# An attention chain with expert routing: rows of x spread by way of DRAM, masks and shares in fewer transfers, part of the first batch on GpSimd, and a new order of work

## The chip, the core and the metric

The kernel runs on one of the eight cores of a Trainium2 chip. A core has five engines that run side by side, each through its own queue in order: TensorE (PE, matrix products; its weight loads are shown as PEld), VectorE (DVE), ScalarE (ACT), GpSimd (POOL) and SyncE (SP), which here issues nearly all the transfers (DMAs). Matrix products land in PSUM, eight banks of 128 x 512 floats; everything else lies in SBUF, 128 rows wide, or in DRAM. The metric is the time of one execution in microseconds (us) of device time; smaller is better.

## The reference

Two blocks follow each other. The first is linear attention with a sketched feature map; its output, with the heads side by side, is the input x of the second, four attention experts of which each token uses two.

```python
# q, k, v: (4 batches, 4 heads, 1088, 32); S1, S2: (8, 32)
phi(x) = outer(S1 @ x, S2 @ x)                     # 64 features per head and row
kv, z  = phi(k)^T @ v, sum(phi(k))
x      = (phi(q) @ kv) / (phi(q) @ z + 1e-6)       # (4, 1088, 128)

logits = x @ w_gate                                # 4 experts
top 2 of each row, w = softmax over those two
for e in range(4):
    a   = softmax(causal((x @ wq[e]) @ (x @ wk[e])^T / 8))
    out += (w of e, or 0) * (a @ (x @ wv[e]) @ wo[e])
```

S1 and S2 come in float64 and are split into two floats at the start.

## The kernel before

The 1088 rows of a batch are nine tiles of 128 (the last has 64). Query times key of an expert is folded into one 128 x 128 matrix per expert (`mcat`), value times output into `mo`, so an expert's scores are x · mcat[e] · x^T. Each row uses two experts, so a tile makes two score rows per token (two "slots"); which expert stands in which slot is a mask, broadcast over all 128 rows of SBUF because the selection runs along the columns. The tiles 0 to 3 are kept in reversed 32-row groups (`BACK`).

There is no automatic scheduling: the text `ORDER` is the program. It is a list of words `batch.task[:arguments]`, executed top to bottom, and each engine's queue holds its instructions in that order. PSUM banks go to the least recently used one (`bank`), with some held over several tasks. A word that needs a result waits on its engine's queue, and everything behind it waits too. The words that matter:

- `ld` loads k, q and v of a batch; `bk`, `bq` transpose k and q on VectorE (for batch 0 the query in halves, `bq0`, `bq1`); `vk` copies the values of batch 0 into `vp`.
- `ks`, `qs` are the sketches: matmuls, a copy on ScalarE, a product. In batch 0 (`first_sketch`, L340) the product reads PSUM and runs on VectorE (L364); in the others it runs on GpSimd (L393).
- `kv` sums the features of k times the values; `tf` turns the query features on PE; `nu` (L415) divides and writes `xs`, one buffer that all batches share; `tx` turns `xs` into `xT` on PE.
- `em`, `eo` fold the expert matrices; `warm` gives PE filler matmuls.
- `ga` computes the gate logits and the selection; `ge` and `gw` the weights. `md` (`spread_masks`, L503) turns the selection, writes it to DRAM (`dm`) and broadcasts it to `mk`. `mp` (`masks`, L522) makes masks of batch 0 on PE instead, before that broadcast is there.
- `cu` (`chosen`, L534) computes x · mcat for two tiles and lets VectorE pick each row's experts by mask (`uT`, L549).
- `s` are scores (L582; the last tile, `last_step`, L604), with mask and maximum on VectorE (L557) and exponentials on ScalarE (L561); `t` transposes the weights on VectorE (L271).
- `sp` (`spread_x`, L274) copies `xs` into `xrep`, which holds x in 32-row blocks, once in each quarter of the rows of SBUF; `vb` and `va` (L638) are the weighted sums over `xrep`, for the tiles 1 to 5 and for 0, 6, 7, 8, in four parts each.
- `shb`, `sha` (`shares`, L654) give the factors of the rows, written to DRAM and broadcast; `shp` does it on PE for the end.
- `zb` sorts the sums by expert (L711, L713), `o` multiplies by `mo` (L720), copies (L723) and stores.

The work of one batch is woven into that of the batch before, so that the start of batch 1 stands among the scores of batch 0. Scores of batch 0 begin after a long chain that has nothing to weave in: sketches, `kv`, `nu`, `tx`, gate, masks, `cu`.

Of the kernel before, what the change touches and what calls it, by code (L numbers as in the profile page):

```python
# [22 lines left out]
    0.bk 0.bq1 0.bq0 0.ks:4:9 0.ks:0:4 0.warm:2 0.qs:0:4 0.warm:2 0.vk 1.ld 0.qs:4:9 0.kv 1.bk 0.tf:0:8 0.warm:2 0.em  # L23
    0.nu:0:4 1.ks:0:4 1.bq 0.tf:13:18 0.tf:8:13 0.tx:0:4 1.ks:4:9 0.nu:4:9 0.eo 0.tx:4:9 0.ga:0:4 0.ge:0 0.gw:0
    0.ga:4:9 1.kv 0.mp:8:9 0.mp:2:4 2.ld 0.ge:4 0.mp:0:2 0.mp:6:8 0.mp:4:6 0.gw:4 2.bk 0.cu:2 1.qs:0:4 1.qs:4:9 0.cu:6
    0.md 0.cu:4 0.cu:0 0.cu:8 1.tf:0:8 1.tf:8:13 0.s:5:1 0.s:3 0.t:1 1.tf:13:18 0.t:5 2.ks:4:9 0.sp 2.ks:0:4 0.s:4:2
    0.s:7 1.nu:5:9 1.nu:0:5 0.shb 0.t:3 2.kv 1.tx:4:9 0.t:4 1.tx:0:4 0.s:8 0.t:2 0.t:7 1.ga:0:9 1.md 0.s:6:0 1.ge:0
    2.bq 0.vb:0 0.vb:1 0.vb:2 0.vb:3 0.zb:5 2.qs:4:9 2.qs:0:4 0.t:0 1.cu:2 0.t:8 0.o:5 1.cu:6 1.cu:4 1.cu:8 0.t:6
    1.cu:0 1.s:4:2 3.ld 3.bk 1.s:5:1 0.sha 0.va:0 0.va:1 1.t:5 2.tf:8:13 2.tf:13:18 0.va:2 1.gw:0 1.t:1 0.zb:3 0.va:3
    0.zb:6 1.sp 2.tf:0:8 1.t:2 1.t:4 1.s:6:0 0.o:3 1.s:3 0.zb:0 0.o:6 0.zb:1 1.s:7 0.o:0 1.t:3 0.o:1 2.nu:5:9 3.ks:4:9  # L30
    3.ks:0:4 2.nu:0:5 1.t:6 1.shb 1.t:7 1.vb:0 0.zb:8 2.tx:0:4 3.bq 2.tx:4:9 1.vb:1 1.vb:2 2.ga:0:9 2.md 2.ge:0 1.vb:3
    0.o:8 3.kv 1.zb:1 1.t:0 1.s:8 3.qs:4:9 3.qs:0:4 2.cu:0 1.o:1 1.t:8 2.cu:4 2.cu:6 1.sha 2.cu:2 2.s:5:1 2.gw:0
    1.zb:5 2.s:3 1.zb:3 1.va:0 1.va:1 2.t:1 1.va:2 1.va:3 1.o:5 3.tf:8:13 3.tf:0:8 2.t:3 3.tf:13:18 2.t:5 2.cu:8
    2.s:4:2 2.t:4 2.sp 1.o:3 2.t:2 2.s:7 2.s:8 1.zb:8 2.shb 3.nu:0:5 3.nu:5:9 1.zb:0 2.vb:0 2.vb:1 2.t:7 3.tx:0:4
    3.tx:4:9 2.vb:2 2.t:8 3.ga:0:9 1.o:8 1.zb:6 3.md 2.vb:3 1.o:0 2.zb:5 2.s:6:0 2.t:6 3.cu:4 1.o:6 2.o:5 3.cu:6
    3.cu:2 3.cu:0 2.zb:1 2.t:0 3.cu:8 3.s:4:2 3.ge:0 3.s:5:1 2.sha 3.t:2 2.zb:3 2.o:1 2.va:0 3.t:1 2.va:1 3.t:4 3.t:5
    2.va:2 2.va:3 2.zb:0 3.s:3 3.sp 3.s:6:0 3.t:0 3.t:3 2.o:3 3.s:7 2.zb:8 3.gw:0 3.shb 2.o:0 3.s:8 2.o:8 3.t:6 3.vb:0
    3.t:8 3.vb:1 3.t:7 3.vb:2 3.vb:3 3.zb:1 3.va:0 3.va:1 3.va:2 3.o:1 3.zb:3 3.shp 2.zb:6 3.va:3 3.o:3 2.o:6 3.zb:6
    3.o:6 3.zb:0 3.zb:5 3.o:0 3.o:5 3.zb:8 3.o:8
# [4 lines left out]
def kernel(  # L44
# [114 lines left out]
    for _ in range(4):  # L159
        nc.tensor.matmul(P[:, 7], idle, idle[:, None, :].to_broadcast([128, 4, 128]), start=True, stop=True)  # L160
# [113 lines left out]
    def spread_x(b):  # L274
        for s in range(4):
            nj = (NC - s + 3) // 4
            for r in range(4):
                nc.sync.dma_start(out=xrep[32 * r : 32 * r + 32, s : s + 4 * (nj - 1) + 1 : 4],  # L278
                                  in_=xs[32 * s : 32 * s + 32, 0:nj])
# [15 lines left out]
    class Batch:  # L295
# [5 lines left out]
        def __init__(self, b):  # L301
            self.b, self.ab, self.fp, self.uT = b, {}, {}, {}
            self.yT, self.qpT = yT, qpT
# [12 lines left out]
    def batch(b):  # L316
        if b not in made:
            made[b] = Batch(b)
        return made[b]
# [20 lines left out]
    def first_sketch(nm, j0, j1, eng):  # L340
# [8 lines left out]
        fp, k0, w = m_.fp[nm], bank(2), 2 * R * (j1 - j0)  # L349
        for j in range(j0, j1):  # L350
# [7 lines left out]
        for m in range(2):  # L358
# [4 lines left out]
            nc.scalar.copy(a, t[:, 0])  # L363
            eng.tensor_tensor(  # L364
                out=o, op=ALU.mult,
                in0=t[:, 1].rearrange("p (j h) r -> p j h r", h=2)[:, :, :, None, :].to_broadcast([128, n, 2, R, R]),
                in1=a.rearrange("p (j h) r -> p j h r", h=2)[:, :, :, :, None].to_broadcast([128, n, 2, R, R]))

    def sketch(b, nm, j0, j1, eng):
        if b == 0:  # L370
            return first_sketch(nm, j0, j1, eng)
# [131 lines left out]
    def spread_masks(b):  # L503
# [7 lines left out]
        for n in range(2):  # L511
            for r in range(4):
                nc.sync.dma_start(out=d[32 * n : 32 * n + 32, r], in_=t8[32 * r : 32 * r + 32, n])
        flat_d = d.rearrange("c r q -> (c r q)")[0 : 2 * X * NJ * 128]
        if b:
            nc.sync.dma_start(out=m_.mk.rearrange("p j x q -> p (j x q)"), in_=flat_d.partition_broadcast(128))
        else:
            for x in (0, 2 * X - 1):
                nc.sync.dma_start(out=m_.mk[:, :, x], in_=flat_d.rearrange("(j x q) -> j x q", x=2 * X, q=128)[:, x]
                                  .partition_broadcast(128))  # L520

    def masks(b, j0, j1):  # L522

        m_, k0 = batch(b), bank(2)
        sb = p2.tile([128, 2, 2 * X], BF16, tag="selb", name=f"selb{b}_{j0}")
# [5 lines left out]
        for j in range(j0, j1):  # L531
            nc.scalar.copy(m_.mk[:, j, 1:5], P[:, k0 + j - j0].rearrange("p (x q) -> p x q", x=4), saturate=False)

    def chosen(b, i):  # L534
# [11 lines left out]
        mk = m_.mk[:, i : i + n, 1:5].rearrange("p t (s x) q -> p t s x q", s=2)[:, :, :, :, 0:q]  # L546
# [107 lines left out]
    def shares(b, grp, by_dma=True):  # L654
# [12 lines left out]
        if by_dma:  # L667
# [3 lines left out]
            for x in range(4):  # L671
                nc.sync.dma_start(out=d[0:n, x], in_=shT[32 * x : 32 * x + n])
# [135 lines left out]
```

## Time and profile before

| | us |
|---|---|
| median of 3 runs (lowest, highest) | 293.4 (291.9, 295.9) |
| the profiled execution | 293.26 |
| its span, first to last instruction | 291.4 |
| PE busy | 269.9 (93%) |
| DVE busy | 220.6 (76%) |
| ACT busy | 105.9 (36%) |
| POOL busy | 53.6 (18%) |
| mean granted PE clock | 0.982 of full |

The profile is one execution. Its span leaves out 1.9 us around the first and last instruction. Busy times come with the number of instructions; a wait is put down to what came last. Lines such as L582 are lines of the kernel before.

### The profile page before, as it was taken

The page shows a single profiled execution, that of the slowest core. Times are in us where ns is not written, and L with a number is a line of the kernel's source. Part 1 is how long each engine was busy: PE and PEld are TensorE (multiplying, and loading weights), DVE is VectorE, ACT ScalarE, POOL GpSimd, SP SyncE. Part 2 cuts the span into 40 slices and gives each one's busy share as a digit, 9 for nine tenths or more (in the row PEclk, how much of TensorE's full clock was granted, in tenths as well). Part 3 has the DMA queues.
Part 4 walks back from the last instruction along what each step waited for, and adds up shares of the span by engine and source line. Part 5 has one row for each costly group of instructions (what it writes and reads, how often), then busy time and mean ns, then how long its engine had stood idle before and what let it go on. Part 6 is the DMA issues. An engine that isn't in the chain of part 4 may idle for free.

```text
span 291.4 us, 10880 instructions
## 1 busy us (share of the span) xinstructions
PE 269.9 (93%) x4661; PEld 215.9 (74%) x4661; DVE 220.6 (76%) x503; ACT 105.9 (36%) x270; POOL 53.6 (18%) x134
## 2 busy tenths in 40 slices
PE   7887599994999999999999699999999999999993
PEld 2766588664489779768889469758888796689992
DVE  6837676973877997898974777888688988779461
ACT  2335174770233254165114142652052432620111
POOL 7016034050022312002323220000300010020100
PEclk9999889997799999999999999999999999999999
DMA  6953200682203801681033010582022024831011
GB/s 209 254 152 92 69 3 3 119 176 56 96 3 124 239 2 49 145 182 48 22 95 121 26 66 4 133 187 109 10 83 77 0 69 99 184 105 64 16 44 42
DMA packets 36616, 26.07 MB, mean 89 GB/s; under 512 B 10200, under 2 KB 34264, under 8 KB 36568
## 3 DMA queue, kind: packets, MB, share of 16 engines
q1 hardware_dynamic: 36552, 25.38, 33.7%
q8 instruction: 36, 0.59, 0.8%
q14 instruction: 12, 0.10, 0.1%
q10 hardware_dynamic: 16, 0.00, 0.0%
HBM read 14.16 MB, written 2.29 MB: 56 GB/s over the span
## 4 chain that ended last, share of the span: by engine, by line
PE 71%; DVE 12%; SPq 5%; DMA 5%; issue 3%; POOL 1%; ACT 1%; DVEq 0%; ACTq 0%; POOLq 0%
PE P L638 22%; PE P L582 18%; PE P L720 9%; PE P L543 9%; SPq L278 4%; PE P L604 3%; PE P L287 2%; PE P L422 2%; DVE aTA L271 2%; PE P L356 2%; DMA mk<-dm 2%; DVE uT L549 1%; DVE qT L332 1%; DVE xs L429 1%; DMA xrep<-xs 1%
## 5 line engine op out<-in xcount | busy, mean ns | idle before, releaser
L561 ACT ACTIVATE a<-a,mx 128x128 f32<-128x128 f32 (+7 forms) x68 | 53.7, 791 | 67.5 <-DVE mx L557 67.2
L582 PE MATMUL P<-xT,uT 128*128 128x512 f32 (+3 forms) x192 | 65.4, 491 | 1.8 <-DVE uT L549 1.8
L582 PEld LDWEIGHTS P<-xT,uT 128*128 128x128 f32 x192 | 33.5, 190 | 27.5 <-issue 20.7
L638 PEld LDWEIGHTS P<-aTA,xrep 32*128 32x128 f32 x1080 | 37.7, 185 | 1.5 <-issue 1.3
L638 PE MATMUL P<-aTA,xrep 32*128 32x160 f32 (+3 forms) x1080 | 38.7, 295 | 0.0
L638 PE MATMUL P<-aTB,xrep 32*128 32x320 f32 (+4 forms) x720 | 37.4, 348 | 0.0
L720 PEld LDWEIGHTS P<-mo,zT 128*128 128x128 f32 (+1 forms) x288 | 33.9, 186 | 3.8 <-issue 1.7
L720 PE MATMUL P<-mo,zT 128*128 128x128 f32 (+1 forms) x288 | 36.0, 278 | 0.4 <-DVE zT L713 0.4
L557 DVE CUSTOM_DVE_ANT_0 a<-P,mask 128x768 f32<-128x768 f32 (+3 forms) x32 | 32.2, 1014 | 4.0 <-PE P L582 4.0
L638 PEld LDWEIGHTS P<-aTB,xrep 32*128 32x128 f32 x720 | 33.2, 186 | 2.8 <-issue 0.3
L543 PE MATMUL P<-xT,mcat 128*128 128x256 f32 (+1 forms) x160 | 33.3, 361 | 0.7 <-DVE uT L549 0.7
L543 PEld LDWEIGHTS P<-xT,mcat 128*128 128x128 f32 x160 | 27.6, 191 | 4.3 <-DVE uT L549 1.1
L549 DVE COPY_PREDICATED uT<-mk,P 128x512 f32<-128x512 uint8 (+1 forms) x40 | 24.8, 638 | 7.0 <-DMA mk<-dm 4.8
L271 DVE STREAM_TRANSPOSE aTA<-a 128x256 f32<-128x256 f32 (+4 forms) x28 | 24.6, 919 | 2.6 <-ACT a L561 2.6
L271 DVE STREAM_TRANSPOSE aTB<-a 128x1024 f32<-128x1024 f32 (+3 forms) x28 | 24.3, 909 | 0.5 <-ACT a L561 0.5
L713 DVE COPY_PREDICATED zT<-mk,yT 128x768 f32<-128x768 uint8 (+2 forms) x24 | 18.6, 774 | 3.2 <-POOL zT L710 0.8
L711 DVE TENSOR_TENSOR zT<-yT,mk 128x768 f32<-128x768 f32 (+2 forms) x24 | 17.1, 714 | 4.3 <-PE P L720 4.0
L723 ACT COPY ob<-P 128x256 f32<-128x256 f32 (+2 forms) x24 | 7.5, 311 | 34.6 <-PE P L720 17.0
L393 POOL TENSOR_TENSOR kp<-kab 128x1024 f32<-128x1024 f32 (+1 forms) x6 | 12.9, 2171 | 25.1 <-DVE kab L390 24.6
L393 POOL TENSOR_TENSOR qp<-qab 128x1024 f32<-128x1024 f32 (+1 forms) x6 | 12.9, 2170 | 15.2 <-DVE qab L390 15.2
L710 POOL MEMSET zT<- 128x256 f32 (+2 forms) x24 | 5.7, 249 | 53.9 <-PE P L720 45.6
L557 DVE CUSTOM_DVE_ANT_0 a<-P,mask_back 128x256 f32<-128x256 f32 (+3 forms) x32 | 15.1, 485 | 0.0
(185 smaller groups left out, 287.7 us busy)
## 6 DMA issues: line engine op xcount, KB each, us to landing
xrep<-xs SPq DMA_DIRECT2D x32, 144.0 KB, 2.9
xrep<-xs SPq DMA_DIRECT2D x32, 128.0 KB, 3.4
mk<-dm SPq DMA_DIRECT2D x3, 864.0 KB, 5.0
kin<-in_k_dram SPq DMA_DIRECT2D x4, 544.0 KB
qin<-in_q_dram SPq DMA_DIRECT2D x4, 544.0 KB
vin<-in_v_dram SPq DMA_DIRECT2D x16, 128.0 KB, 5.2
out_dram<-ob SPq DMA_DIRECT2D x16, 64.0 KB, 2.3
out_dram<-ob SPq DMA_DIRECT2D x64, 16.0 KB, 1.5
```

Of the source, the lines that this page charges most:

```text
L271: nc.vector.transpose(t[:, 0 : c1 - c0, n - u0 : n - u0 + s].rearrange("p c s k -> p s c k"), a[:, :, 32 * c0 : 32 * c1].rearrange("p s (c ...
L278: nc.sync.dma_start(out=xrep[32 * r : 32 * r + 32, s : s + 4 * (nj - 1) + 1 : 4], in_=xs[32 * s : 32 * s + 32, 0:nj])
L393: eng.tensor_tensor(out=fp[:, j0:j1].rearrange("p j h (x y) -> p (j h) x y", y=R), in0=a_[:, 1, :, None, :].to_broadcast([128, n, R, R]), ...
L543: nc.tensor.matmul(P[:, k0 + x // 2, x % 2 * w : x % 2 * w + w], mcat[:, e], queries, start=True, stop=True)
L549: nc.vector.copy_predicated(u, mk[:, :, :, x].bitcast(U8), c[:, :, None].to_broadcast([128, n, 2, q]))
L557: nc.vector.tensor_tensor_reduce(out=dst, in0=src, in1=msk, scale=-1.0, scalar=most, op0=ALU.add, op1=ALU.min, accum_out=mx)
L561: nc.scalar.activation(out=a, in_=a, func=ACTF.Exp, bias=mx, scale=-1.0, accum_out=z)
L582: nc.tensor.matmul(flat[:, f + c : f + c + n], turned(b, i)[:, s], m_.xT[:, c - at[i] : c - at[i] + n], start=True, stop=True)
L638: nc.tensor.matmul(P[:, sums[grp][r], 32 * us[0] : 32 * len(units)], xrep[rows, c], t[rows, c - c0, us[0] - u0 :], start=(c == 0), stop=(c ...
L711: nc.vector.tensor_tensor(out=z[:, :, 0:X], in0=y[:, :, 0, None].to_broadcast([128, n, X, nq]), in1=mk[:, :, 0:X], op=ALU.mult)
L713: nc.vector.copy_predicated(z[:, :, 1:], mk[:, :, X:].bitcast(U8), y[:, :, 1, None].to_broadcast([128, n, X, nq]))
L720: nc.tensor.matmul(P[0:nq, k0, DM * t : DM * t + DM], self.zT[:, t, e], mo[:, e], start=(e == 0), stop=(e == E - 1))
```

## The change

Its parts:

1. `spread_x` no longer copies each of four groups of rows four times from SBUF (16 transfers). It writes the four groups to a DRAM tile `dx` and reads that back four times, each time into one quarter of the rows of `xrep` (8 transfers).
2. `spread_masks` writes the turned selection with four transfers instead of eight, and broadcasts all of it for batch 0 too. The masks that PE makes for batch 0 go to a tile of their own, `mp`, which shares the two buffers of the tag `mk`, with one copy per two tiles instead of one per tile.
3. `shares` writes its factors with one transfer instead of four; the broadcast tile has the quarters outermost, so its rows in DRAM are shorter.
4. In batch 0, GpSimd copies the values (`vk`), and multiplies the second half of the query features; for those ScalarE copies a second operand out of PSUM.
5. One fp32 filler matmul is dropped at the start; the order has ten bf16 fillers where it had six.
6. `ORDER` is new throughout. In batch 0: the values before the queries; `tf:0:8` before `kv`; both `nu` and `sp` at once after it; the gate of the tiles 0 to 3 alone, then their masks and `cu`, before the gate of the others. `sp` of batch 0 stood among its scores and stands ahead of its gate now. At the end, `o` of the tiles 3 and 5 of batch 3 stands ahead of `va:3`.

```diff
@@ ORDER (its first lines)
-    0.bk 0.bq1 0.bq0 0.ks:4:9 0.ks:0:4 0.warm:2 0.qs:0:4 0.warm:2 0.vk 1.ld 0.qs:4:9 0.kv 1.bk 0.tf:0:8 0.warm:2 0.em
-    0.nu:0:4 1.ks:0:4 1.bq 0.tf:13:18 0.tf:8:13 0.tx:0:4 1.ks:4:9 0.nu:4:9 0.eo 0.tx:4:9 0.ga:0:4 0.ge:0 0.gw:0
-    0.ga:4:9 1.kv 0.mp:8:9 0.mp:2:4 2.ld 0.ge:4 0.mp:0:2 0.mp:6:8 0.mp:4:6 0.gw:4 2.bk 0.cu:2 1.qs:0:4 1.qs:4:9 0.cu:6
-    0.md 0.cu:4 0.cu:0 0.cu:8 1.tf:0:8 1.tf:8:13 0.s:5:1 0.s:3 0.t:1 1.tf:13:18 0.t:5 2.ks:4:9 0.sp 2.ks:0:4 0.s:4:2
+    0.bk 0.vk 0.warm:2 0.warm:2 0.bq0 0.bq1 0.ks:4:9 1.ld 0.qs:0:4 0.warm:2 0.ks:0:4 0.qs:4:9 0.tf:0:8 0.kv 1.bk
+    0.tf:13:18 0.tf:8:13 0.nu:0:4 0.nu:4:9 0.sp 0.tx:0:4 1.bq 0.warm:2 0.warm:2 0.tx:4:9 0.ga:0:4 1.ks:4:9 1.ks:0:4
+    0.em 0.mp:2:4 0.mp:0:2 0.ge:0 0.gw:0 0.cu:0 0.cu:2 0.ga:4:9 1.kv 1.qs:4:9 1.qs:0:4 0.eo 2.ld 0.mp:6:8 0.mp:4:6
+    0.mp:8:9 0.cu:4 2.bk 1.tf:13:18 0.cu:6 1.tf:8:13 0.s:4:2 1.tf:0:8 0.s:3 1.nu:5:9 0.t:2 2.ks:4:9 2.ks:0:4 0.t:4
...
@@ ORDER (from va:3 of batch 2, and the last lines)
-    2.va:2 2.va:3 2.zb:0 3.s:3 3.sp 3.s:6:0 3.t:0 3.t:3 2.o:3 3.s:7 2.zb:8 3.gw:0 3.shb 2.o:0 3.s:8 2.o:8 3.t:6 3.vb:0
-    3.t:8 3.vb:1 3.t:7 3.vb:2 3.vb:3 3.zb:1 3.va:0 3.va:1 3.va:2 3.o:1 3.zb:3 3.shp 2.zb:6 3.va:3 3.o:3 2.o:6 3.zb:6
-    3.o:6 3.zb:0 3.zb:5 3.o:0 3.o:5 3.zb:8 3.o:8
+    2.va:2 2.va:3 3.sp 3.t:1 2.o:3 2.o:5 3.s:3 2.zb:8 3.s:6:0 3.t:3 3.s:7 3.s:8 3.vb:0 3.gw:0 3.vb:1 3.vb:2 3.t:0
+    3.shb 3.t:7 3.t:8 2.o:8 3.t:6 3.vb:3 3.va:0 3.va:1 3.va:2 2.zb:0 2.o:0 3.zb:3 3.shp 3.o:3 3.zb:1 3.o:1 3.zb:5
+    3.o:5 2.zb:6 3.va:3 3.zb:0 2.o:6 3.o:0 3.zb:6 3.o:6 3.zb:8 3.o:8
@@
-    for _ in range(4):
+    for _ in range(3):
         nc.tensor.matmul(P[:, 7], idle, idle[:, None, :].to_broadcast([128, 4, 128]), start=True, stop=True)
@@ spread_x
+        d = dp.tile([32, NC, DM], F32, tag="dx", name=f"dx{b}")
         for s in range(4):
             nj = (NC - s + 3) // 4
-            for r in range(4):
-                nc.sync.dma_start(out=xrep[32 * r : 32 * r + 32, s : s + 4 * (nj - 1) + 1 : 4],
-                                  in_=xs[32 * s : 32 * s + 32, 0:nj])
+            nc.sync.dma_start(out=d[:, s : s + 4 * (nj - 1) + 1 : 4], in_=xs[32 * s : 32 * s + 32, 0:nj])
+        for r in range(4):
+            nc.sync.dma_start(out=xrep[32 * r : 32 * r + 32], in_=d)
@@ first_sketch
             nc.scalar.copy(a, t[:, 0])
+            second, eng = t[:, 1], nc.vector
+            if nm == "q" and m:
+                second, eng = other[:, 2 * j0 : 2 * j1], nc.gpsimd
+                nc.scalar.copy(second, t[:, 1])
             eng.tensor_tensor(
...
@@ spread_masks
-        for n in range(2):
-            for r in range(4):
-                nc.sync.dma_start(out=d[32 * n : 32 * n + 32, r], in_=t8[32 * r : 32 * r + 32, n])
-        flat_d = d.rearrange("c r q -> (c r q)")[0 : 2 * X * NJ * 128]
-        if b:
-            nc.sync.dma_start(out=m_.mk.rearrange("p j x q -> p (j x q)"), in_=flat_d.partition_broadcast(128))
-        else:
-            for x in (0, 2 * X - 1):
-                nc.sync.dma_start(out=m_.mk[:, :, x], ...
+        for r in range(4):
+            nc.sync.dma_start(out=d[:, r].rearrange("(n c) q -> c n q", n=2), in_=t8[32 * r : 32 * r + 32])
+        nc.sync.dma_start(out=m_.mk.rearrange("p j x q -> p (j x q)"),
+                          in_=d.rearrange("c r q -> (c r q)")[0 : 2 * X * NJ * 128].partition_broadcast(128))
@@ masks
+        if m_.mp is None:
+            m_.mp = p2.tile([128, NJ, 4, 128], F8, tag="mk", name=f"mp{b}")
...
-        for j in range(j0, j1):
-            nc.scalar.copy(m_.mk[:, j, 1:5], P[:, k0 + j - j0].rearrange("p (x q) -> p x q", x=4), saturate=False)
+        nc.scalar.copy(m_.mp[:, j0:j1].rearrange("p j x q -> p (j x q)"), flat[:, 512 * k0 : 512 * (k0 + j1 - j0)], saturate=False)
@@ shares
-            d = dp.tile([10, 4, 32], F32, tag="ds", name=f"ds{b}{grp}")
-            for x in range(4):
-                nc.sync.dma_start(out=d[0:n, x], in_=shT[32 * x : 32 * x + n])
-            nc.sync.dma_start(out=t[:, 0:n].rearrange("p u r q -> p (u r q)"),
-                              in_=d.rearrange("u r q -> (u r q)")[0 : 128 * n].partition_broadcast(128))
+            d = dp.tile([128, 32], F32, tag="ds", name=f"ds{b}{grp}")
+            nc.sync.dma_start(out=d, in_=shT)
+            nc.sync.dma_start(out=t[:, :, 0:n].rearrange("p r u q -> p r (u q)"),
+                              in_=d.rearrange("(r u) q -> r (u q)", r=4)[:, 0 : 32 * n].partition_broadcast(128))
@@ values_of_k
-        nc.scalar.copy(vp[:, 0 : NJ - 1, :, 0:D].rearrange("p j h d -> p h j d"), vin)
-        nc.scalar.copy(vp[0:64, NJ - 1, :, 0:D], vtl)
+        nc.gpsimd.tensor_copy(vp[:, 0 : NJ - 1, :, 0:D].rearrange("p j h d -> p h j d"), vin)
+        nc.gpsimd.tensor_copy(vp[0:64, NJ - 1, :, 0:D], vtl)
```

## The prediction

> **What bounds it now.** I read the page's busy table and slices first, then TensorE's waits, then the timeline at each wait.
>
> ```profile
> span 291.4 us, 10880 instructions
> PE 269.9 (93%) x4661; PEld 215.9 (74%) x4661; DVE 220.6 (76%) x503; ACT 105.9 (36%) x270; POOL 53.6 (18%) x134
> PEclk9999889997799999999999999999999999999999
> ```
>
> TensorE (PE) is busy for 269.9 of 291.4 us, so nearly all that can be won lies in its 21.5 idle us and in the stretches where its granted clock (PEclk) is below 9. Who kept it idle (sum, times, longest):
>
> ```profile
> PE P L287 <- DVE xs L429: 4.8, 3, 4.1
> PE P L529 <- DVE selb L526: 3.5, 1, 3.5
> PE P L582 <- DVE uT L549: 1.8, 2, 1.6
> ```
>
> The first, in the timeline: the queue of SyncE (SPq), then VectorE (DVE), then PE. Two-microsecond windows (columns: PE, PEld, DVE, ACT, POOL, clock, DMA share, GB/s) show the rest.
>
> ```profile
> 52.94 13.13 SPq L278 DMA_DIRECT2D xrep<-xs  x16
> 69.44 0.76 DVE L429 TENSOR_TENSOR xs<-P,den 128x256 f32<-128x256 f32 x2 [4.80 <-DMA xrep<-xs]
> 71.57 1.23 PE L287 MATMUL P<-ident,xs 64*128 64x64 f32 x18 [4.13 <-DVE xs L429]
> 72.72 3.59 PE L604 MATMUL P<-xT,uT 128*64 128x64 f32 x12
> ...
> 192.86 2.06 PE L604 MATMUL P<-xT,uT 128*64 128x64 f32 x12
> ```
> ```profile
> 32.00:34.00 2.00, 0.00 (x0) 0.00 (x0) 1.37 (x7) 0.00 (x0) 0.39 (x2) 1.00 0.00 0
> 36.00:38.00 2.00, 2.00 (x21) 2.00 (x20) 0.78 (x5) 2.00 (x6) 0.00 (x0) 0.50 0.02 4
> 58.00:60.00 2.00, 2.00 (x8) 1.16 (x7) 2.00 (x7) 0.84 (x3) 1.87 (x1) 1.00 1.06 190
> 70.00:72.00 2.00, 0.43 (x8) 0.43 (x10) 1.74 (x7) 0.00 (x0) 0.00 (x0) 0.50 0.00 0
> ```
>
> Sixteen transfers read `xs`, so batch 1 cannot overwrite it until 69.44, and PE idles 4.13 us. The clock then falls to 0.50: the same `last_step` matmuls take 3.59 us instead of 2.06, the transposes 1.23 instead of 0.78. The place costs 4.13 + 1.53 + 0.45 = **6.1 us**. The second place is 31.5 to 34.95: VectorE chews both gate halves before the first mask matmul, PE idles 3.5 us, and the 36 mask matmuls run at a low clock (3.78 us). The rest: 2.5 us at 162 to 169.5 (masks of batch 2 land late), and 4.9 us from the last matmul (286.5) to the end.
>
> **The start, walked with the rows of before.** From the first scores on, PE has the same work in both kernels, so a microsecond won ahead of them lasts to the end unless a new wait takes it. I go through both engines in the new order, each step at the duration of its row. Until VectorE has `kT` (7.9) nothing changes; one fp32 filler less and two more pairs of bf16 fillers ahead of it fill a wait. `qT` is ready at 7.82 + 2.20 = 10.0. PE (144 records of L356 take 2.35): ks:4:9 to 9.2, wait 0.8, qs:0:4 to 11.1, two fillers 0.6, ks:0:4 to 12.8, qs:4:9 to 14.1, tf:0:8 0.7, kv 2.3 to 17.1, the other tf 0.8, both nu 1.1 + 1.35, to 20.5 (before: 25.5). VectorE ends `xs` at 20.5 + 1.4 = 21.9, then 1.bq (2.2, L332), the gate of four tiles (28.79 to 30.6, so 1.8), four kab additions (1.0), two selb (0.25): 27.1. Sixteen mask matmuls: 3.78 us for 36 at half clock gives 0.055 each at full, 0.9. The first `chosen` starts at 28.0, where before it started at 38.56. Left until the first scores (L582): cu:0, cu:2 (3.6), ga 0.45, kv 2.3, qs 1.25, eo 1.1 and its two waits 0.5, 20 mask matmuls 1.1, cu:4 and cu:6 3.6, tf 0.8, and 0.8 for mask copies that ScalarE does behind `mo`: **43.5** against 48.8. Cu:8 and two features come later than before (0.95 + 0.2). Net **-4.1**. The idle gaps left are under 1 us, shorter than the 3.5 that preceded a clock drop; if one such gap came back it would cost 3.5 + 1.9.
>
> Parts hidden inside that walk. Values by GpSimd: 1.06 + 0.29 leave ScalarE (L743), GpSimd does the same copy in 1.06 + 0.29 (L323) and had nothing else from 6.5; kv needs it at 14.8, so even data landing at 12 is in time; later, each us is a us. Query products by GpSimd: VectorE loses 0.70 + 0.82 (L364), ScalarE gains 0.22 + 0.23, GpSimd's rows (1951 ns for 1024, 2390 for 1280, 1.71 ns an element) give 1.08 and 1.29, ending at 12.9 and 16.0 against needs at 14.1 and 17.5: nothing.
>
> [...] This trace has 2390 ns for 1280. [...]
>
> **x through DRAM.** The four reads of `xs` go out at 21.9 for batch 0: 4 x 0.65 (L278) + 2.9 to landing, free at 27.4; the next writer of `xs` comes at about 50. The 6.1 us go: **-6.1**. It is moved ahead of 2.ld's eight loads on SyncE's queue, which now wait until about 30 for the four wide transfers; kT of batch 2 is read at 43, and kin landed within 5 us, so 8 us of cover. For batches 1 to 3 the four DRAM reads wait on the last weighted sum (va:3). No row shows a 32-partition read of long rows, so bounds: 2.23 MB at 190 GB/s (the window at 58, 512-byte rows) is 11.7 us, at 408 GB/s (4 to 6 us, the input loads) 5.5; with landing 1.5, 13.2 or 7. I take the slow end, since the window is the same destination. PE's cover between va:3 and the next vb:0: in batch 3, 2.68 (o:3, o:5) + 1.72 + 3.51 + 3.44 (scores) + 1.98 = 13.3; before batches 1 and 2 about 17.5 and 18. So -0 to +2 at one place: **+0.5**.
>
> [...]
>
> **Masks and shares.** One transfer per quarter instead of two saves 4 x 0.45 us on the way gate to masks (3.56 for eight). Before, that way took batch 2 from 146.7 to 161.3. In the new order batch 2's must wait for 0.zb:6, which waits for 0.o:8: from there zb 2.0, turning 0.5, four issues 1.8, landing 3.0, broadcast 4.7, 12.0 in all, while PE does vb:2 and vb:3 (4.1), qs 1.2, s:7 3.44, cu:2 and its copy 2.3: 11.0, so 1 us late. In batch 3 gate and the same way take 4.2 + 9.5 = 13.7 against 2.4 + 2.6 + 2.0 + 0.9 + 1.5 + 1.2 = 10.6: 3 late, of which other work of PE hides one. PE loses 0.4 + 2.0 against 2.5: **0**; from -2.5 to +3 if the ways differ by 3 us. Batch 0's masks in one tile: nine copies (4.6) become five of about 1.0 and 0.6, on ScalarE, hidden behind `chosen`'s 1.7 us of matmuls a pair; uncovered, the 0.8 in the walk is what they cost. The second mask tile takes a slot of `mk`, so the broadcast of batch 1 (about 77) waits for 0.cu:8, done by 53: nothing. The yT products read their shares in another order; L644's 620 and 820 ns stand for both layouts, from nothing to as much again, hidden on VectorE except for the last one (1.16 us before the end). Shares: 4 issues become 1, 1.05 us off a transfer needed 7 us later; broadcast rows a quarter as long could cost its 3.5 us again and still be in time.
>
> **End.** o:3 and o:5 of batch 3 move ahead of va:3. After va:3 VectorE makes yT 1.16, zb:0 1.15, zb:6 2.0; o:0 and o:6 wait for it 0.65 + 1.1, against 0.4 before; but the last copy no longer waits for a buffer (1.85, L723). **0**.
>
> **Middle.** By task sums from the rows, VectorE has about as much to do as PE between the first scores and 3.kv (some 75 against 81 us), and the 4.13 us idle were also its time to catch up. New short waits for banks of PSUM: from 0 to 5; I take **+1**, as DVE's slices there stand at 7 to 9.
>
> Sum: -4.1 - 6.1 + 0.5 + 0 + 0 + 1.0 = -8.7. The profiled execution took 293.26 (1.9 around the span) and agrees with the median of 293.4: **284.5 us**.
>
> **Rivals.**
> A, forecast, 282 to 287: chance 0.52.
> B, VectorE takes the place of the stalls: of the 6.1 at the `xs` wait about 4 come back as PE waiting for uT or banks between 50 and 100. For: the near tie. Against: VectorE was idle 4.8 us itself before 69.44. 289; 0.22.
> C, better: xrep at 408 GB/s, no mask wait, no bank waits: 284.5 - 0.5 - 2.4 - 1.0, and less: 280; 0.13.
> D, the other side: xrep lands late in every batch. The DMA order decides, at va:3's end. With covers 17.5, 18, 13.3, landing after 19.2 us (130 GB/s) eats the 8.7. At 110 GB/s it lands after 22, late by 4.5, 4 and 8.7, each with a dropped clock (2 us): 284 + 23 = 307. Against: 190 measured. 0.06.
> E, it doesn't do what it says: `xs` is still held by a later wait on the queue and the first masks still come late: 292; 0.07.
>
> Two per cent is about what a measurement tells from no change. Faster by over 2% (under 287.5) are nearly all of A, C and a little of B: 0.67; within: 0.26; slower: 0.07. The range leaves out D, E and the tail of C: 279 to 291.
>
> **What would show it.** The first matmuls of `chosen` near 28 and the first scores near 43; no wait of PE for `xs` above 1; no 7 or 8 in PEclk after slice 4; the wide xrep transfers landing in under 13.5 us; PE's remaining waits on uT in batches 2 and 3. Wrong if PE waits for VectorE between 50 and 100, or the weighted sums wait for xrep.

## The result, and the profile after

The changed kernel takes 307.8 us (median of 4 runs, 305.4 to 309.3) against 293.6 (291.9 to 295.9) for the kernel before on the same chip: a ratio of 1.047, interval 1.037 to 1.058. It is slower, where 284.5 us was forecast. Medians are of all executions, ratios and their intervals of the fast ones alone; of four kernels below (the two in the old order with new parts, and the first and last on the casts) the profiled execution was a slow one, so their traces serve for durations and waits only.

The page of the changed kernel: span, TensorE's line, the granted clock in 40 slices.

```profile
span 307.1 us, 10806 instructions
PE 280.8 (91%) x4663; PEld 222.4 (72%) x4663; DVE 226.2 (74%) x501; ACT 105.9 (35%) x266; POOL 57.6 (19%) x138
PEclk9975689999999999969999999999999999999999
```

TensorE's busy time rose by 10.9 us with the same work but for the fillers, and its idle time from 21.5 to 26.3. Part of the busy time that is more is clock: 5 to 8 stand in slices 2 to 5 (counted from 0) and a 6 in slice 18. Windows on TensorE (busy, clock, DMA share, GB/s) put the low clock in three places:

```profile
20.00:30.00 10.00, 10.00 (x257) 0.50 0.19 46
33.40:40.20 6.80, 5.96 (x26) 0.50 1.08 238
132.40:139.20 6.80, 4.38 (x53) 0.50 0.27 55
```

Half of the busy time at half clock makes 10.2 us, as an estimate. In the kernel before, with 3.35 us busy from 34.9 to 38.3 and 4.33 from 69.0 to 75.9, the same sum makes 3.8. So some 6.3 of the 10.9 us are clock; section 7 comes back to the rest.

Its waits in the changed kernel (sum, times, longest):

```profile
PE P L721 <- issue: 5.7, 1, 5.7
PE P L531 <- DVE selb L528: 4.2, 3, 1.7
PE P L412 <- issue: 2.4, 1, 2.4
PE P L583 <- DVE uT L550: 2.3, 2, 1.4
```

The wait for `xs` is gone. The first and third line are new and have no releaser: "issue" means that TensorE waited for nothing that the profile names. In the timeline both break off a group of matmuls in its middle, and SyncE's queue (SPq) shows what had been handed to the DMA engines shortly before:

```profile
10.49 2.57 SPq L120 DMA_DIRECT2D vin<-in_v_dram  x4
...
18.73 1.40 PE L412 MATMUL P<-vp,kp 128*64 128x33 f32 x37 [2.44 <-issue]
...
122.79 1.90 SPq L280 DMA_DIRECT2D xrep<-dx  x4
...
128.37 0.78 PE L721 MATMUL P<-mo,zT 128*128 128x128 f32 x5
...
134.82 2.71 PE L721 MATMUL P<-mo,zT 128*128 128x128 f32 x11 [5.67 <-issue]
```

Five of sixteen equal matmuls run, then nothing for 5.67 us, then eleven at half clock. What came in between stands in the DMA view, which counts packets by queue. Its queue q8 ("instruction") moves 36 packets, 0.59 MB, in the whole span, and TensorE has 9,326 records: 259 for each 16 KB packet. All other engines together have fewer than 1,500. So these are TensorE's own instructions. The first line below is from 124.5 to 132, where q8 has none; the next two from 132 to 134.8.

```profile
q1 hardware_dynamic: 141, 1.67, 104.8%
```
```profile
q1 hardware_dynamic: 142, 0.36, 66.3%
q8 instruction: 1, 0.02, 3.1%
```

For 7.5 us all sixteen DMA engines were full with the four reads of x; the block of instructions came at 132.06, took 1.38 us, and TensorE went on 1.4 us later. At the start it is the same: from 11.8 to 15.9 no packet on q8 under a DMA share of 104%, then one at 15.95, which took 1.35 us, and kv goes on at 18.73, 1.4 us later again. The places of the breaks fit too. Counting all of TensorE's records in the trace, its sequencer's among them, kv breaks off after 705 and L721 after 4,545: each 193 more than a multiple of 256. So do its three smaller waits without a releaser (after 1,729, 4,033 and 4,289), and none of those of over 0.3 us that have one.

### The profile page after: what moved, and what is told of

It reads as the page before. It is cut to its first block, busy times and chain, and to the rows that moved or that the text cites. A ratio compares the mean times of both kernels' runs of the same rounds, so it can differ in the third digit from the quotient of the medians.

```text
span 307.1 us, 10806 instructions
## 1 busy us (share of the span) xinstructions
PE 280.8 (91%) x4663; PEld 222.4 (72%) x4663; DVE 226.2 (74%) x501; ACT 105.9 (35%) x266; POOL 57.6 (19%) x138
## 4 chain that ended last, share of the span: by engine, by line
PE 59%; DVE 21%; DMA 8%; issue 6%; POOL 2%; SPq 1%; ACT 0%; DVEq 0%; POOLq 0%; ACTq 0%
PE P L583 20%; PE P L639 11%; PE P L544 7%; PE P L721 6%; PE P L428 3%; PE P L288 3%; PE P L412 3%; DMA mk<-dm 3%; DVE aTA L271 3%; DVE zT L712 3%; DVE zT L714 3%; DMA dm<-sel 2%; DVE uT L550 2%; DMA sbc3B<-ds3B 2%; DVE selb L528 2%
## 5 line engine op out<-in xcount | busy, mean ns | idle before, releaser
L562 ACT ACTIVATE a<-a,mx 128x640 f32<-128x640 f32 (+8 forms) x68 | 53.8, 792 | 51.8 <-DVE mx L558 50.8
L721 PE MATMUL P<-mo,zT 128*128 128x128 f32 (+1 forms) x288 | 38.3, 286 | 6.4 <-issue 5.7
L721 PEld LDWEIGHTS P<-mo,zT 128*128 128x128 f32 (+1 forms) x288 | 34.8, 191 | 10.7 <-issue 8.4
L639 PE MATMUL P<-aTA,xrep 32*128 32x160 f32 (+3 forms) x1080 | 39.8, 296 | 1.0 <-issue 1.0
L558 DVE CUSTOM_DVE_ANT_0 a<-P,mask 128x640 f32<-128x640 f32 (+3 forms) x32 | 32.3, 1013 | 5.3 <-PE P L583 5.3
L639 PEld LDWEIGHTS P<-aTB,xrep 32*128 32x128 f32 x720 | 33.4, 185 | 3.9 <-issue 1.3
L544 PE MATMUL P<-xT,mcat 128*128 128x256 f32 (+1 forms) x160 | 35.6, 377 | 0.0
L544 PEld LDWEIGHTS P<-xT,mcat 128*128 128x128 f32 x160 | 29.2, 200 | 4.6 <-issue 0.5
L550 DVE COPY_PREDICATED uT<-mk,P 128x512 f32<-128x512 uint8 (+1 forms) x30 | 18.5, 637 | 6.0 <-DMA mk<-dm 5.5
L399 POOL TENSOR_TENSOR kp<-kab 128x1280 f32<-128x1280 f32 (+1 forms) x6 | 12.9, 2170 | 40.4 <-DVE kab L396 40.4
L558 DVE CUSTOM_DVE_ANT_0 a<-P,mask_back 128x384 f32<-128x384 f32 (+3 forms) x32 | 15.5, 487 | 2.8 <-PE P L583 2.8
L399 POOL TENSOR_TENSOR qp<-qab 128x1280 f32<-128x1280 f32 (+1 forms) x6 | 12.9, 2172 | 20.8 <-DVE qab L396 20.8
```

The lines of the kernel that those rows point to most:

```text
L399: eng.tensor_tensor(out=fp[:, j0:j1].rearrange("p j h (x y) -> p (j h) x y", y=R), in0=a_[:, 1, :, None, :].to_broadcast([128, n, R, R]), ...
L544: nc.tensor.matmul(P[:, k0 + x // 2, x % 2 * w : x % 2 * w + w], mcat[:, e], queries, start=True, stop=True)
L550: nc.vector.copy_predicated(u, mk[:, :, :, x].bitcast(U8), c[:, :, None].to_broadcast([128, n, 2, q]))
L558: nc.vector.tensor_tensor_reduce(out=dst, in0=src, in1=msk, scale=-1.0, scalar=most, op0=ALU.add, op1=ALU.min, accum_out=mx)
L562: nc.scalar.activation(out=a, in_=a, func=ACTF.Exp, bias=mx, scale=-1.0, accum_out=z)
L639: nc.tensor.matmul(P[:, sums[grp][r], 32 * us[0] : 32 * len(units)], xrep[rows, c], t[rows, c - c0, us[0] - u0 :], start=(c == 0), stop=(c ...
```

## The experiments

**Theory F**: a block of TensorE's instructions waits behind bulk transfers on the DMA engines, TensorE runs dry, and the clock falls behind the gap. **Rivals**: the new order itself (O), something else in the stretch at 129 (M). Each kernel was run beside the kernel before; ratios are to it.

**1. The first batch's values.** In the changed kernel, ScalarE again, behind the third fillers:

```
-    0.bk 0.vk 0.warm:2 0.warm:2 0.bq0 0.bq1 0.ks:4:9 1.ld 0.qs:0:4 0.warm:2 0.ks:0:4 0.qs:4:9 ...
+    0.bk 0.warm:2 0.warm:2 0.bq0 0.bq1 0.ks:4:9 0.qs:0:4 0.warm:2 0.ks:0:4 0.vk 1.ld 0.qs:4:9 ...
-        nc.gpsimd.tensor_copy(vp...
+        nc.scalar.copy(vp...
```

> The changed kernel, with the copy of the first batch's values back on ScalarE, as in the kernel before, and put behind the third warm-up, so that the value loads of batch 1 are issued later (13.2 us in the kernel before, 10.5 in the changed one). Theory F (fetch): TensorE's own instructions come in blocks of 16 KB over the DMA engines; in the changed kernel a block that TensorE asked for at about 12.7 us came only at 15.95 to 17.30, behind the early loads of batch 1, kv stood 2.44 us and the granted clock was 0.50 from 19.8 to 30. With the loads later, F expects kv to stand under 1 us (0.63 in the kernel before), the clock at 20 to 30 us back near 1.0, the first scores at 47 to 51 us instead of 56.4, and 298 to 303 us in all. Rival O (order): the low clock and the late start come from the new order of the start (masks waiting for VectorE, gate pieces between), whatever the loads do: first scores stay at 54 to 57, and 305 to 309 us in all.

304.7 us, 1.033 (1.023 to 1.043), 3.1 less than the changed kernel, with intervals that overlap; section 6 has this edit again, clear of noise. The kv group runs without its gap. But the clock was 0.66 both from 10 to 20 and from 30 to 40, and the first scores came at 55.2, as O had it: F was right on the stall, wrong that the clock and the scores would follow. The stall before L721 stayed (5.8). When TensorE asked for the late block, 12.7 us in the expectation, stands in no view: it was the author's estimate.

**2. The sixteen direct transfers back**, alone and with edit 1:

```
-        d = dp.tile([32, NC, DM], F32, tag="dx", name=f"dx{b}")
...
+            for r in range(4):
+                nc.sync.dma_start(out=xrep[32 * r : 32 * r + 32, s : s + 4 * (nj - 1) + 1 : 4],
+                                  in_=xs[32 * s : 32 * s + 32, 0:nj])
```

> The changed kernel with the sixteen direct transfers of x in place of the way through DRAM, at the new places in the order. Theory F: the block of TensorE's instructions that came at 132.06 was held up behind the four reads of x from DRAM, whose 128 packets of 17 KB take 1.36 us each; so the stall of 5.67 us before 134.8 and the low clock from 132.4 to 139.2 go, the start stays as it is (kv stands about 2.4 us, first scores near 56), and the whole takes 298 to 302 us. Rival M: the stall at 129 comes from something else in that stretch (the order of the output tasks, the masks, the shares' load), and stays: 306 to 311 us. A third outcome: the sixteen transfers take SP 12 to 13 us in each batch, as before, and a new wait for x or for the outputs' buffers of 2 to 5 us takes the stall's place: 302 to 306.

> Both edits of the two kernels above together: the changed kernel with the first batch's values by ScalarE and x by sixteen direct transfers; left of the change are the masks and shares in fewer transfers, half the query features' product by GpSimd and the new order. Theory F: both losses go, 288 to 294 us, TensorE without an idle time over 2 us behind the loads of the start. Rivals O and M together: above 302 us. If only one of them holds, 296 to 303.

324.7 us, 1.107 (1.097 to 1.118), and 320.1, 1.086 (1.077 to 1.096). No expectation held. The stall without a name at 129 is gone, but this says nothing of F, for a larger one stands in its place. TensorE's waits in the first of the two:

```profile
PE P L543 <- DVE xs L434: 10.8, 1, 10.8
PE P L582 <- DVE xs L434: 8.3, 1, 8.3
```

The new order writes `xs` for the next batch right behind the spreading of x; it needs the early release that the way through DRAM gives.

**3. Half of the reads**, in batch 1 alone:

```
-        for r in range(4):
+        for r in range(2 if b == 1 else 4):
             nc.sync.dma_start(out=xrep[32 * r : 32 * r + 32], in_=d)
```

> The changed kernel without two of the four reads of x from DRAM in batch 1 alone (half of the copies of x are left out there, so batch 1's result is not the reference's; every other instruction stays, TensorE's stream too). Theory F: the block of TensorE's instructions that came at 132.06 waited for the reads that were issued before it; with half of them the DMA engines are through some 5 us earlier, the stall of 5.67 us falls below 1.5 us, the low clock behind it goes, and the whole takes 299 to 302.5 us. Rival M (the stall has another cause in that stretch): a stall of 4 us or more stays at 127 to 135 us, and 305 to 309 us in all.

303.6 us, 1.028 (1.023 to 1.033), 4.2 less. The same sixteen matmuls:

```profile
127.48 0.78 PE L721 MATMUL P<-mo,zT 128*128 128x128 f32 x5
130.37 2.71 PE L721 MATMUL P<-mo,zT 128*128 128x128 f32 x11 [2.11 <-issue]
```

TensorE runs dry at the same instruction, and the gap is 2.1 us in place of 5.7 (under 1.5 expected): the block comes as the reads end, here at 127.6. M falls: half the cause gives 3.6 us less stall. The clock still fell behind the gap: eleven matmuls take 2.71 us here, sixteen 2.19 at full clock in section 5.

**4. The shape of the reads.** Four reads by columns, each for all 128 partitions, in the changed kernel and in the kernel before:

```
-        for r in range(4):
-            nc.sync.dma_start(out=xrep[32 * r : 32 * r + 32], in_=d)
+        for c0, c1 in ((0, 9), (9, 18), (18, 26), (26, NC)):
+            nc.sync.dma_start(out=xrep[:, c0:c1], in_=d[None, :, c0:c1].to_broadcast([4, 32, c1 - c0, DM]))
```

> The changed kernel with the four reads cut the other way: each reads a quarter of the columns for all 128 partitions (packets of 4 to 4.6 KB) in place of all columns for 32 partitions (packets of 17 KB at 1.36 us, 12.8 GB/s for one DMA engine). The loads of k in the changed kernel, 128 partitions with packets of 4.4 KB, took 168 ns at the median, 26 GB/s. So F expects the four reads to be through in 5 to 7 us in place of 11, TensorE's late block at 132 to come 4 to 5 us earlier, the stall of 5.67 us to fall under 2 us: 299 to 303 us. If it is the number of bytes alone that counts (11 us whatever the rows) the stall stays over 4 us and the time at 305 to 309.

> The kernel before with x by way of DRAM at the old places (302.9 us with 32-partition reads, TensorE 3.8 us idle for late x in three batches and 2.2 us for a late block of its instructions), the reads cut by columns as above. F expects the waits for x to go (the reads end 4 to 5 us earlier) and the fetch stall to shrink under 1 us: 289 to 296 us. If what made this variant slow was the low clock of its first 80 us (7.2 us against 2.7), which the reads' shape does not touch: 299 to 303.

324.5 us, 1.098 (1.091 to 1.105), and 334.3, 1.137 (1.130 to 1.144). The expectation was wrong in the rate. A window of the first during its reads (busy of PE, PEld, DVE, ACT, POOL; clock, DMA share, GB/s):

```profile
140.00:145.00 5.00, 5.00 (x115) 3.26 (x106) 3.48 (x14) 2.42 (x6) 2.69 (x5) 1.00 0.31 118
```

The DMA engines are 31% busy at 118 GB/s, against 223 and a full share with the large reads (1.67 MB in the 7.5 us above): as much as five of sixteen at work. Why so few share reads of this shape was not shown. The reads lasted some 19 us, and outputs behind them on the queue held up ScalarE and TensorE for up to 11.9 us. So the two runs say nothing of F.

**5. The reads in sixteen pieces**, each 32 partitions by a quarter of the columns. SyncE hands them over in 9.98 us, about as fast as they are moved: a piece landed 4.2 to 4.4 us after its issue (medians), a large read 10.7 in the changed kernel. So fewer should stand ahead of a block of instructions.

```
+        for c0, c1 in ((0, 9), (9, 18), (18, 26), (26, NC)):
+            for r in range(4):
+                nc.sync.dma_start(out=xrep[32 * r : 32 * r + 32, c0:c1], in_=d[:, c0:c1])
```

> The changed kernel with each of the four reads of x from DRAM in four pieces (sixteen reads of 32 partitions by a quarter of the columns, 4 to 4.6 KB a packet; same bytes). SP issued such pieces every 0.51 us in the run with reads by columns, so sixteen take some 8.5 us to issue, near the 10.9 us that the four large ones take to move: the reads are handed over about as fast as they are done, and few of them stand ahead of a block of TensorE's instructions. Theory F: the stall of 5.67 us at 129 falls under 1.5 us, the low clock behind it goes, 298 to 303 us. Rival B (what counts is only that the DMA engines are full, whatever is queued): the block comes when the reads are done, the stall stays over 3.5 us, 304 to 309.

302.3 us, 1.031 (1.024 to 1.037), 5.5 less than the changed kernel, all bytes and instructions of TensorE the same. SyncE's issues and the matmuls that had been broken:

```profile
119.63 9.98 SPq L281 DMA_DIRECT2D xrep<-dx  x16
...
126.64 2.19 PE L722 MATMUL P<-mo,zT 128*128 128x128 f32 x16
```

Sixteen matmuls in one go, at full clock (1.00 in the windows from 125 to 129). The block that TensorE had lacked came at 125.04, with the reads still going and the DMA engines 0.97 busy from 125 to 127. So it was not full engines alone that held it up; that it was what stood queued ahead of it is F's reading, and agrees: F holds, B falls. The same pair in the kernel before, with the old order: x through DRAM with four large reads, then with sixteen.

> The kernel before with one part of the change alone: x by way of DRAM, at the places that the old order has for it. Theory F: the wait of 4.1 us for xs at 67.4 goes, or nearly, but the four reads of 17 KB rows fill the DMA engines for some 11 us in each batch, and wherever TensorE asks for its next block of instructions in that time it stands still without a named cause, at least once for over 1 us: 287 to 295 us. Rival H (the reads harm nothing; the changed kernel's loss is all in its order): 285 to 288 us with no idle time on TensorE over 1 us that has no named cause, outside the first 20 us.

> The kernel before with x by way of DRAM in all batches at the old places, read in sixteen pieces as above. It was 302.9 us with four large reads. F: the wait for xs of 4.1 us goes as it did there, and the late blocks of instructions (2.2 us, 2.1 us) and the low clock behind them do not come: 286 to 293 us. Rival B: 299 to 304 us, with idle times over 2 us on TensorE near 65 and 200 us.

302.9 us, 1.031 (1.023 to 1.039), slower than F and H had it, and 291.4, 0.991 (0.986 to 0.995), as F had it. The pieces alone are worth 11.5 us here. With large reads TensorE's waits had these, which are gone with the pieces:

```profile
PE P L639 <- DMA xrep<-dx: 3.8, 3, 1.7
PE P L423 <- issue: 2.2, 1, 2.2
```

The second is a late block too: it begins after 2,497 records, again 193 more than a multiple of 256. The first is weighted sums that wait for x itself, so the 11.5 us are not the instruction stream's alone.

**6. What is left: order by parts.** Both cures in the changed kernel; and, all with x in sixteen pieces and the first values by ScalarE, the other corners of old and new order by old and new parts (masks and shares in fewer transfers, query products by GpSimd).

> The changed kernel with both cures: reads of x in sixteen pieces, and the first batch's values by ScalarE (that alone gave 304.7 us). F: the two add up, 295 to 300 us; still not below the kernel before (293 to 295), since the start of the changed kernel lost clock in every run of it so far (4 to 7 us against 1.7). Rival B: 301 to 306.

> Old order; all new functions (masks and shares in fewer transfers, half the first query features' product by GpSimd), with x read in sixteen pieces and the first batch's values by ScalarE. It stands to the kernel with both cures (298.3 us, new order) by the order alone, and to the kernel before with x in sixteen pieces (291.4 us) by the functions alone. Theory W (what is left of the loss is the new order): 289 to 294 us. Rival P (it is in the new functions): 296 to 301 us.

> The new order with the old functions (masks, shares, query products and the first values as in the kernel before), x read in sixteen pieces. Theory W: the order carries what is left of the loss, 296 to 300 us, with the same three waits for the masks' numbers at 30 to 52 us. Rival P: 289 to 294 us.

| | old parts | new parts |
|---|---|---|
| old order | 291.4, 0.991 (0.986 to 0.995) | 292.5, 0.989 (0.981 to 0.998) |
| new order | 296.9, 1.010 (1.005 to 1.015) | 298.3, 1.014 (1.006 to 1.021) |

The cures add up: from 307.8 the pieces take 5.5 us, the values by ScalarE another 4.0. The corners are near W's numbers. The new parts cost nothing that can be told apart; the new order costs 5.5 to 5.9 us by the medians and 5.6 to 7.1 by the ratios. Both cures leave one late block, of 1.3 us at L640, with the clock at 0.50 from 118.6 to 128.8 behind it; the kernel with the new order and old parts has no such wait of over 0.5 us and full clock from 48.3 on, and is slower than its twin in the old order all the same. The order without the cures:

> The changed kernel with the old order of tasks: all new functions (x by way of DRAM, fewer transfers of masks and shares, values and half the first query features by GpSimd), none of the moves. If the new order carries a loss of its own (rival O), this comes out near the old kernel with DRAM alone, 300 to 304 us, or better. If the new order is a gain that the fetch stalls hide (F), this is as slow as the changed kernel or slower: 304 to 310 us, with waits for x at the weighted sums in two or three batches as in the old kernel with DRAM alone.

304.9 us, 1.025 (1.018 to 1.032). The median lies between the two; the ratio, 0.022 under the changed kernel's 1.047 but from two executions, puts the order's cost near 6 us here too, as rival O had it. F's stall is there as well, at another place: TensorE waits 4.2 us at L428 with no releaser, again after 2,497 records, and 3.5 us for x at the weighted sums.

**7. Why the order costs.** The casts of the selection to bf16 (`selb`) that the first masks wait for. Line views of the kernel before and of the changed one (min, median, max in ns):

```profile
L526 DVE CAST selb<-sel x5: 165/174/175, 34.7 to 37.3; 128x12 bf16<-128x12 f32 x4, 128x6 bf16<-128x6 f32 x1
```
```profile
L528 DVE CAST selb<-sel x5: 159/1198/2249, 32.0 to 50.2; 128x12 bf16<-128x12 f32 x4, 128x6 bf16<-128x6 f32 x1
```

An operation of 0.17 us takes up to 2.25. GpSimd (POOL) and VectorE in the changed kernel:

```profile
31.76 4.30 POOL L399 TENSOR_TENSOR kp<-kab 128x1280 f32<-128x1280 f32 x2 [10.39 <-DVE kab L396]
```
```profile
31.99 2.26 DVE L528 CAST selb<-sel 128x12 bf16<-128x12 f32 x2
34.17 0.16 DVE L491 TENSOR_REDUCE top<-lg 128x4 f32<-128x16 f32 x1
34.36 1.73 DVE L492 TENSOR_TENSOR w<-lg,top 128x16 f32<-128x16 f32 x1
```

The first product takes 2.39 us by its row (L393 of the kernel before) and so ends at 34.15; the held cast ends at 34.18. The second ends at 36.06, and L492, 0.17 us in the kernel before, ends at 36.09. The reduction between, 0.16 us, is not held. So a cast and a subtraction each ended 0.03 us after the end of a GpSimd product; what makes them wait and spares the reduction was not shown. Theory H: the new order lays the casts on these products. First the casts went to ScalarE, with both cures and in the changed kernel alone:

```
-        nc.vector.tensor_copy(sb[:, 0 : j1 - j0]...
+        nc.scalar.copy(sb[:, 0 : j1 - j0]...
```

> The kernel with the new order and both cures (298.3 us), with one more edit: the five casts of the selection to bf16 that the first masks wait for go to ScalarE. Theory H (held): in the changed kernel two of these casts on VectorE took 2.19 and 2.25 us where they take 0.17, and each ended 0.03 us after the end of a sketch product on GpSimd; the new order lays them on top of these products, and TensorE waits for them three times, 4.2 us in all. H expects the waits for selb to fall below 1 us together, the first scores from 50.8 to 46 to 48.5, and 292 to 296 us in all. Rival G (the masks are late because VectorE is late with the gate, whoever casts): waits for selb of 2.5 us or more stay, and 297 to 300 us.

> The changed kernel itself with the five casts on ScalarE and nothing else altered. H: 303 to 305.5 us, with the late block of instructions at 129 and its stall of 5 to 6 us as they were. Rival G: 306.5 to 309 us.

299.7 us, 1.021 (1.016 to 1.025), and 312.0, 1.067 (1.059 to 1.075): no gain, the second 4 us slower. The casts take 0.2 us, but on ScalarE three of the five stand behind the mask copy (1.0 us) of the task before and two behind a copy of expert matrices (0.6), and TensorE waits five times. In the second kernel:

```profile
PE P L531 <- ACT selb L528: 5.2, 5, 1.2
```

Then the casts on VectorE and the mask tasks ahead of batch 1's sketches:

```
-    ... 0.ga:0:4 1.ks:4:9 1.ks:0:4 0.em 0.mp:2:4 0.mp:0:2 0.ge:0 ...
+    ... 0.ga:0:4 0.em 0.mp:2:4 0.mp:0:2 1.ks:4:9 1.ks:0:4 0.ge:0 ...
-    ... 1.kv 1.qs:4:9 1.qs:0:4 0.eo 2.ld 0.mp:6:8 0.mp:4:6 0.mp:8:9 0.cu:4 ...
+    ... 1.kv 0.eo 2.ld 0.mp:6:8 0.mp:4:6 0.mp:8:9 1.qs:4:9 1.qs:0:4 0.cu:4 ...
```

> The kernel with the new order and both cures (298.3 us), with the casts on VectorE and the order altered at two places: the first two and the last three mask tasks stand ahead of batch 1's key and query sketches, so that the casts run before GpSimd starts its products of 2.39 and 1.91 us. Theory H: the casts take 0.17 us again, the waits for selb fall from 3.7 us to under 1.5, the first scores come at 47.5 to 49.5 in place of 50.8, and the whole takes 294 to 296.8 us. The other side (the hold is real but hides behind something else, as it did when ScalarE made the casts): the casts are short, but another wait of 2 us or more stands in the first 52 us, and the time stays at 297 to 300.

299.7 us, 1.012 (1.005 to 1.020), no different from the kernel it was made of (1.014). All five casts take 0.17 us, and TensorE waits 3.5 us for them all the same, 2.6 at one place: the subtraction of L492 (2.00 us) and the product behind it (1.62) are held instead, and VectorE comes late to the second half of the gate. The hold is shown; its price is not, as each way out made a new wait of its size.

The start is also not where the order loses most of its 5.5 us. In the two kernels with old parts, old order and then new, the first scores come at 50.70 and 51.59. From there to the last matmul (busy of PE, PEld, DVE, ACT, POOL; clock, DMA share, GB/s):

```profile
50.70:285.05 234.35, 229.28 (x3675) 183.08 (x3671) 186.88 (x397) 85.83 (x217) 36.26 (x94) 1.00 0.36 96
51.59:292.26 240.67, 233.30 (x3689) 184.74 (x3685) 189.64 (x409) 87.01 (x219) 36.27 (x96) 1.00 0.29 82
```

At full clock in both, the new order takes 6.3 us longer here: 2.3 more idle and 4.0 more busy, of which about 1 is work that it puts off (the first batch's last `cu` and some turns of features). The other 3 are the same matmuls at the same clock, which keep TensorE busy longer. So of the order's cost only 0.9 us lay in the start, where the casts are. Why the same matmuls take longer in the new order stays open.

**8. What can be had.** The kernel before, x through DRAM in sixteen pieces in batch 0 alone; then with the fewer transfers of masks and shares as well.

```
     def spread_x(b):
+        if b:
+            return spread_direct(b)   # the sixteen transfers of before
```

> The kernel before with x by way of DRAM in sixteen pieces in batch 0 alone, where xs is waited for; batches 1 to 3 keep the sixteen direct transfers. F: the one wait of 4.1 us and its low clock of two windows (69.05 to 75.87) go, nothing else moves: 286 to 291 us. Rival B: a late block of instructions near 62 to 68 us takes the wait's place: 291 to 296 us.

> The kernel before with x by way of DRAM in sixteen pieces in batch 0 alone (289.3 us), and the masks and shares in fewer transfers; old order, everything else old. Theory W: the fewer transfers save SP some 0.4 us for each of 30, but SP bounds nothing here: 287 to 290 us, no change that a run can show. Rival P: the one mask load of 0.86 MB for batch 0, against two of 0.14, delays a block of TensorE's instructions or the copies of x: 291 to 296 us.

289.3 us, 0.984 (0.976 to 0.991), and 287.5, 0.977 (0.971 to 0.982): both kernels of the case are beaten, by 7.1 us the old one. The page of the last:

```profile
span 285.7 us, 10834 instructions
PE 270.1 (95%) x4661; PEld 216.1 (76%) x4661; DVE 220.9 (77%) x503; ACT 105.8 (37%) x266; POOL 53.7 (19%) x134
PEclk9999989999999999999979999999999999999998
```

Idle time is 15.6 us in place of 21.5, and the low clock behind the `xs` wait is gone. The intervals of the two runs overlap, so the fewer transfers are at best a small gain.

## Why the prediction was wrong

In the profiled executions half of the error lies ahead of the first scores, which came 12.9 us later than forecast. The other half lies behind them: 247.2 us from there to the last matmul against 238.0 before, where the terms of the sum make it 4.6 less and the work put off 1.2 more.

From kernel to kernel the difference reads: before 1.000; x through DRAM in pieces 0.991; the new order 1.010; the new parts 1.014; the values by GpSimd 1.031; the reads in four large transfers 1.047.

- **The stall at `xs`, -6.1: right.** Gone in the changed kernel; taken away alone in batch 0 it is worth 5.1 us (289.3 against 294.4).
- **Values by GpSimd, "even data landing at 12 is in time": the step that failed first.** The copy was in time, 9.37 to 10.65. But it gave `vin` free, so batch 1's value loads went out at 10.49 in place of 13.24, onto engines still busy with k and q (a share of 104% from 11.8 to 15.9), and TensorE's next block came at 15.95, where it came at 14.53 in the kernel before. kv stood 2.44 us, and the clock was 0.50 from 19.8 to 30.0. The copy was costed by its own rows; what its early end sets off was not asked. With the reads in pieces it costs 4.0 us (302.3 against 298.3).
- **x through DRAM, +0.5: the place was right, the victim was not.** The reads behaved as bounded: first issue 122.79, over at about 136, by the slow end (13.2 us); no weighted sum of batches 1 to 3 waits for them, so rival D did not come. That D's 307 is near the measured 307.8 is chance. What waited was TensorE's instruction stream, which no term and no rival held: 5.67 us and a low clock, 5.5 us in all by the pair of runs (11.5 in the old order, where the weighted sums waited too). Batches 2 and 3 escaped: around their reads (from 193.8 and from 256.4) blocks came at 193.8 and 205.8, and at 255.9 and 273.1, and TensorE waited for none.
- **The start, -4.1: wrong also without the stalls.** The first `chosen` came at 35.9 (forecast 28.0, before 38.6), the first scores at 56.4 (43.5, 48.8). With both cures they are at 31.6 and 50.8: the scores still later than before. Mis-sized were "two selb (0.25)", which took 2.26 us under GpSimd's product, and "the idle gaps left are under 1 us": three waits for selb, 4.2 us. The clock at the start, taken as full, cost 7.7 us of busy time up to 60 us (windows of 10 us, busy times one minus clock; 1.1 in the kernel before).
- **Masks late, 0: right.** Waits of 2.3 us for uT in batches 2 and 3 against 2.4 forecast and 2.5 before. The fewer transfers and the query products cost nothing that a run can tell.
- **Middle, +1: too small, and of another kind.** Rival B did not come: between 57 and 120 us TensorE waits once for VectorE, 0.7 us. But "From the first scores on, PE has the same work in both kernels" did not mean the same busy time. Behind the first scores TensorE was busy 235.3 us against 230.5, with 2.2 us lost to the clock in each and about 1 us of work put off; without the late blocks the order costs 6.3 us there, that work included (section 7).

## What to carry to other kernels

A bulk transfer can have one more victim than the code shows: the instruction stream, which stood 5.67 us here. Where a tuned kernel hands the DMA engines several microseconds of work at once (7.5 us of full engines here), look for matmul groups broken in their middle with no named releaser, and hand the work over in pieces at the rate at which it is moved. When an engine gets faster, follow the buffer that it frees and the transfer that starts earlier; and when a small VectorE operation is moved, see whether GpSimd is at work there: a cast of 0.17 us took up to 2.25 here. Before curing a loss, compare the kernels stretch by stretch: the place that looks worst need not be where they differ.

## What the runs showed of the hardware

- TensorE's instructions come as packets of 16 KB (36 in the changed kernel), one for 259 of its records, 0.9 to 1.9 us each. Where one was late TensorE stopped at a fixed count, 193 more than a multiple of 256 of its records in each of the breaks counted here, and went on 1.4 to 1.6 us after the packet's end. Under a full queue of reads one came 2.9 us after TensorE had run dry, when the reads were nearly through. At two places of the changed kernel the wait was 2.4 and 5.7 us.
- Reads of 17 KB rows to 32 partitions moved at 223 GB/s with the engines full (104.8% from 124.5 to 132 in the changed kernel); with a repeat of four outermost they moved at 118 GB/s at a share of 0.31 (section 4, from 140 to 145).
- In the changed kernel and the one before, the granted clock was 1.0 or 0.5 in stretches of 3.4 us or multiples of it (0.5 from 19.8 to 30.0, 33.4 to 40.2 and 132.4 to 139.2 in the changed one, from 34.9 to 38.3 and 69.0 to 75.9 before). The kernel of section 1 and the one with both cures have the same start; from 10 to 20 us the first ran at 0.66, after 1.9 us of waiting for the query, the second at 1.00, after 0.7. By the sum of windows above, the kernel before and its variants in section 8 lost 1.1 to 2.4 us up to 60 us, kernels with the new order 2.9 to 10.5, and the kernel before with x through DRAM in four reads 4.2. What decides was not tried.
